# First transform stages of h and K: two matmuls of 64 rows on the two halves of the array's rows, in place of two of 128 rows with zeros

## The chip, the core and the metric

The kernel runs on one core of a Trainium2 chip. The core has TensorE (PE; its weight loads are shown apart as PEld), VectorE (DVE), ScalarE (ACT), GpSimd (POOL) and SyncE (SP), which here only issues DMAs. SBUF is the working memory of 128 partitions, and PSUM, in banks of 128 x 512 f32, takes the results of matmuls. The metric is the device time of one launch in microseconds, lower is better.

## The reference, cut to what matters

One layer with two blocks, on 2048 positions of width D = 640. The change lies in the first block:

```python
h = _layernorm(x) * (1 + ca) + sa
# A block: a long convolution along the positions, for each of the 640 channels
P = exp((A * dt)[:, :, None] * pos)           # 640 x 128 x 2048
K = 2.0 * einsum("dn,dnl->dl", C, P).real     # the filter, 640 x 2048
y = irfft(rfft(h, 2L) * rfft(K, 2L), 2L)[:L]  # + h * D_skip
x = x + ga * y
# B block: x = x + gb * ((silu(h2 @ w1) * (h2 @ w3)) @ w2), h2 a layernorm of x
```

The kernel computes the Fourier transforms as matmuls in stages. The change concerns the first stage of the transform of h and the first stage of that of K.

## The kernel before, in words

Positions are split into 32 outer (t1) and 64 inner (t0) ones. The first stage is a transform over the 32 outer positions, which gives 32 frequencies with a real and an imaginary part, 64 numbers. A tile holds four groups of 32 positions on its 128 partitions (q = 0 to 3). One matmul handles two groups: its 128 output rows are 64 numbers for one group and 64 for the other. The weights for a pair of groups (`pr`, line 268 for h and 574 for K) have 128 rows, and in `shape_tables` only the 64 rows that belong to the pair are filled: rows 0 to 63 for pr = 0, rows 64 to 127 for pr = 1. The others are zeros.

**h.** `h_unit` (lines 248 to 272) does one of eight units: two inner positions j of each group. DVE applies the layernorm to the unit's tile xs (lines 258 and 261, one instruction each for each j), SP loads the unit's weights wa (L254), and then for each pr a tile ho (128 x 2 x 640) is filled: for each j and each half of 320 columns one f32 matmul into a PSUM tile of tag "f" (L268), and an ACT copy from there into ho (L269). Then two DMAs write ho to h1 in DRAM (L272). Buffers: four of xs (XB), two of wa, three of ho (HB), three PSUM tiles of tag "f" (self.fb), which other matmuls share.

**K.** The filter is generated in five pieces of 128 channels (`gen_steps`, `gen_chunk`: POOL and DVE multiply tables, ACT takes sines in lines 489 to 495, PE sums over the 128 states in line 511 into kps, and ACT copies it to ks, L532). `k_steps` (lines 551 to 584) then runs the first transform stage on a piece, in four stages of 16 inner positions: for each pr one f32 matmul of 512 columns (L574), an ACT copy into the tile ko (L576), and after both two DMAs to k1 in DRAM (L581). For the first four pieces each matmul has a PSUM tile "f" of its own. For the last one (`wide`) both write one PSUM tile of two banks (tags "sn" and "cs"), which one ACT instruction copies (L578). ko has two buffers (KB).

`freq_steps` (lines 597 to 630) reads h1 and k1 back (ht and kt, L594) and does the second transform stage (L612 for h, L626 for K), the product on DVE (L628), and the first stage of the inverse (L616). All these have weights of 128 x 128. The second stage of the inverse (L655, and L927 for the first units) uses weights of 128 rows and 64 columns, two matmuls at a time into the two halves of PSUM's partitions (`tile_position`). After this comes the B block (`ffn`), from about 600 us to the end.

**The order of the work** isn't written out by hand. Each step has a priority (`self.at(...)`), and when the program is built a list scheduler with modelled times fixes the order on each engine; on the chip each engine takes its instructions in that order and waits by semaphore. In the h stage the generation of K's first piece runs between the units of h. Some orders are pinned by `self.order`: the h normalisations follow one another on DVE, and the sines on ACT. SP's queue holds the loads of xs, wa and K's parameters and the writes of ho and ko, in one line.

Of the kernel before, what the change touches and what calls it, by code (L numbers as in the profile page):

```python
# [10 lines left out]
F32 = mybir.dt.float32  # L11
F32R = mybir.dt.float32r
I32 = mybir.dt.int32
AF = mybir.ActivationFunctionType
# [4 lines left out]
P = 128  # L19
L = 2048  # L20
D = 640
# [17 lines left out]
HB = int('3')  # L39
# [59 lines left out]
class K:  # L99
# [148 lines left out]
    def h_unit(self, e, ps, u):  # L248
        nc = self.nc
        j0 = u * 2  # L250
        rstd, nm = self.h_rs
        xs = self.xs[u] or self.load_x(e, u, "xs")
        wa = e.tile([P, 2, 2, P], F32, name=f"wa{u}", tag="wa", bufs=2)
        nc.sync.dma_start(wa, self.t_wa[:, j0:j0 + 2])  # L254
        for j in range(2):
            x = xs[:, j, :]
            c = slice(j0 + j, j0 + j + 1)
            i0 = nc.vector.scalar_tensor_tensor(x, x, nm[:, c], self.rA, op0=ALU.add, op1=ALU.mult)  # L258
            if self.hq:
                self.order(i0, self.hq[-1])  # L260
            i0 = nc.vector.scalar_tensor_tensor(x, x, rstd[:, c], self.rB, op0=ALU.mult, op1=ALU.add)
            self.hq.append(i0)
        for pr in range(2):
            ho = e.tile([P, 2, D], F32, name=f"ho{u}{pr}", tag="ho", bufs=HB)
            for j in range(2):
                for o in (0, 320):
                    pt = ps.tile([P, 512], F32, name=f"ph{u}{pr}{j}{o}", tag="f", bufs=self.fb)
                    nc.tensor.matmul(pt[:, :320], wa[:, j, pr, :], xs[:, j, o:o + 320], start=True, stop=True)  # L268
                    nc.scalar.activation(ho[:, j, o:o + 320], pt[:, :320], AF.Copy)  # L269
            for g in range(2):  # L270
                t0 = 16 * (2 * pr + g) + j0
                nc.sync.dma_start(self.h1.rearrange("f r t d -> (f r) t d")[:, t0:t0 + 2, :], ho[g * 64:(g + 1) * 64])  # L272


    def params_begin(self, e):
# [275 lines left out]
    def k_steps(self, pc, st, kop, ps, bufs, wide=None):  # L551

        nc = self.nc
        o0, E, SB = pc * P, E4, 16

        dsk = kop.tile([P, E], F32, name=f"dsk{pc}", tag="dsk", bufs=2)
        nc.gpsimd.memset(dsk, 0.0)
        for q in range(4):
            o = o0 + (2 * (q % 2) + q // 2) * E
            nc.sync.dma_start(dsk[32 * q:32 * q + 1], self.d_skip[o:o + E].rearrange("(o e) -> o e", o=1))  # L560

        def stage(i):
            ks = st["ks"]
            if i == 64 // SB - 1:
                nc.vector.tensor_add(ks[:, 63, :], ks[:, 63, :], dsk)
            ko = (wide if wide and i == 2 else kop).tile([P, SB, 2 * E], F32, name=f"ko{pc}{i}", tag="ko", bufs=1 if wide and i == 2 else bufs)
            kv = ko.rearrange("p s (r e) -> p r s e", r=2)
            if wide:
                pt = ps.tile([P, 2, SB, E], F32, name=f"pk{pc}{i}", tag=("sn", "cs")[i % 2], bufs=1)
            for pr in range(2):  # L570
                if not wide:
                    pt = ps.tile([P, 1, SB, E], F32, name=f"pk{pc}{i}{pr}", tag="f", bufs=self.fb)
                pv = pt[:, pr if wide else 0]
                nc.tensor.matmul(pv, self.wk[:, pr, :], ks[:, i * SB:(i + 1) * SB, :], start=True, stop=True)  # L574
                if not wide:
                    nc.scalar.activation(kv[:, pr], pv, AF.Copy)  # L576
            if wide:
                nc.scalar.activation(kv, pt, AF.Copy)  # L578
            for g in range(2):
                o = o0 + 2 * g * E  # L580
                nc.sync.dma_start(self.k1.rearrange("f r s d -> (f r) s d")[:, i * SB:(i + 1) * SB, o:o + 2 * E],  # L581
                                  ko[g * 64:(g + 1) * 64])

        return [lambda i=i: stage(i) for i in range(64 // SB)]


# [404 lines left out]
```

## Time and profile before

| | us |
|---|---|
| median of 3 runs | 1206.31 (1205.34 to 1208.49) |
| the profiled execution | 1206.96 |
| its span, first to last instruction | 1205.2 |
| PE busy | 1029.8 (85%) |
| DVE busy | 696.6 (58%) |
| ACT busy | 495.2 (41%) |
| POOL busy | 316.6 (26%) |
| L268, matmuls of h, busy in the h stage (83 to 172) | 51.4 |
| L574, matmuls of K, busy | 42.2 |

A busy time is the time in which at least one instruction of the kind ran. "out<-in" names tiles by the program's names: ph and pk are the PSUM tiles of the two first stages, ho and ko the SBUF tiles they are copied to, h and k the DRAM tensors h1 and k1. A number with x counts instructions. "<-" behind an idle time names what ended it. PEclk is the granted clock of TensorE, 1.00 or in tenths of full speed. A line that says "issue" stands for time in which the engine waited for nothing that the profile shows.

### The profile page before, as it was taken

What the parts mean: (1) busy time and instruction counts of PE and PEld (TensorE: products, weight loads), DVE (VectorE), ACT (ScalarE), POOL (GpSimd) and SP (SyncE); (2) the same over time, 40 slices, a digit from 0 to 9 for tenths busy, and PEclk for the clock granted to TensorE, in tenths of its full rate; (3) what the DMA queues carried; (4) which work ended last, traced back from release to release, by engine and by line L of the source; (5) the groups of instructions that cost most, each with busy time, mean ns of one, the idle gap of its engine ahead of it and who ended that gap; (6) DMA issues with size and microseconds to landing.
All of it is one profiled execution on the core that took longest, in us unless ns stands there. A gap on an engine that the chain in (4) does not pass through costs nothing.

```text
span 1205.2 us, 17828 instructions
## 1 busy us (share of the span) xinstructions
PE 1029.8 (85%) x6737; PEld 777.4 (65%) x6737; DVE 696.6 (58%) x1224; ACT 495.2 (41%) x768; POOL 316.6 (26%) x329
## 2 busy tenths in 40 slices
PE   2357673895996989895699999999999999999996
PEld 0134342673775857674376788888888888888885
DVE  7999979746866763143474484544745445354332
ACT  3456566436456573312242243432424333343221
POOL 5677768645757871000000000000000000000000
PEclk9578785797897988998699999999999999999999
DMA  9957648335365454778956333533335332353311
GB/s 265 232 160 222 184 125 220 86 104 116 95 172 112 114 117 122 175 187 218 214 142 155 97 88 88 136 96 86 97 88 133 108 95 74 84 143 98 98 44 44
DMA packets 206525, 157.61 MB, mean 131 GB/s; under 512 B 56680, under 2 KB 188648, under 8 KB 204776
## 3 DMA queue, kind: packets, MB, share of 16 engines
q1 hardware_dynamic: 206440, 156.48, 49.8%
q8 instruction: 53, 0.87, 0.3%
q14 instruction: 32, 0.26, 0.1%
HBM read 119.74 MB, written 36.70 MB: 130 GB/s over the span
## 4 chain that ended last, share of the span: by engine, by line
PE 70%; DVE 14%; DMA 7%; ACT 3%; issue 2%; SPq 2%; POOL 1%; DVEq 0%; ACTq 0%
PE gu L760 11%; PE gu L758 10%; PE gu L759 10%; PE fk L626 6%; PE fa L616 5%; PE acc L793 5%; PE acc L795 5%; PE acc L794 5%; PE fa L612 3%; PE kps L511 3%; PE iy L655 2%; DMA k<-ko 1%; DMA xt<-in_x 1%; DVE xs L258 1%; DVE step L446 1%
## 5 line engine op out<-in xcount | busy, mean ns | idle before, releaser
L758 PE MATMUL gu<-xh,wh 128*128 128x512 f32 x540 | 214.2, 397 | 0.5 <-ACT xh L695 0.5
L760 PE MATMUL gu<-xh,wl 128*128 128x512 f32 x540 | 213.9, 396 | 0.0
L759 PE MATMUL gu<-xl,wh 128*128 128x512 f32 x540 | 213.9, 396 | 0.0
L670 ACT ACTIVATE wh<-wr 128x640 fp32r<-128x640 f32 x108 | 74.2, 732 | 146.7 <-PE gu L759 134.5
L511 PE MATMUL kps<-yy,xx 128*32 128x64 f32 x2560 | 83.5, 247 | 53.3 <-DVE xx L503 28.3
L511 PEld LDWEIGHTS kps<-yy,xx 128*32 128x32 f32 x2560 | 61.6, 123 | 101.4 <-issue 53.9
L727 POOL MEMSET w2l<- 64x640 f32 x4 | 2.5, 626 | 469.0 <-PE acc L794 469.0
L758 PEld LDWEIGHTS gu<-xh,wh 128*128 128x128 f32 x540 | 101.7, 188 | 26.1 <-issue 1.0
L760 PEld LDWEIGHTS gu<-xh,wl 128*128 128x128 f32 x540 | 101.5, 188 | 26.4 <-issue 2.0
L759 PEld LDWEIGHTS gu<-xl,wh 128*128 128x128 f32 x540 | 101.6, 188 | 24.9 <-issue 0.5
L628 DVE TENSOR_TENSOR fp<-fk,hz 128x512 f32<-128x512 f32 x80 | 54.8, 686 | 98.1 <-PE fk L626 97.8
L626 PE MATMUL fk<-kt,wb 128*128 128x128 f32 x640 | 99.8, 305 | 13.1 <-DMA kt<-k 12.3
L626 PEld LDWEIGHTS fk<-kt,wb 128*128 128x128 f32 x640 | 90.6, 212 | 23.8 <-DMA kt<-k 7.6
L793 PE MATMUL acc<-ah,w2h 128*128 128x512 f32 x260 | 104.6, 402 | 0.0
L794 PE MATMUL acc<-ah,w2l 128*128 128x512 f32 x260 | 102.7, 395 | 0.0
L618 ACT ACTIVATE hz<-fa 128x512 f32<-128x512 f32 (+1 forms) x90 | 49.2, 547 | 126.5 <-PE fa L616 105.6
L487 POOL TENSOR_TENSOR yy<-e,e 128x512 f32<-128x512 f32 x80 | 87.0, 1109 | 42.7 <-PE kps L511 42.7
L795 PE MATMUL acc<-al,w2h 128*128 128x512 f32 x260 | 98.1, 395 | 0.0
L671 DVE TENSOR_TENSOR wl<-wr,wh 128x640 fp32r<-128x640 f32 x108 | 84.5, 817 | 16.6 <-ACT wh L670 16.6
L773 DVE SCALAR_TENSOR_TENSOR a<-th,gu 128x512 f32<-128x512 f32 x52 | 35.7, 687 | 100.3 <-ACT th L772 100.2
L774 DVE TENSOR_TENSOR a<-a,gu 128x512 f32<-128x512 f32 x52 | 35.7, 686 | 94.5 <-PE gu L760 94.5
L772 ACT ACTIVATE th<-gu 128x512 f32<-128x512 f32 x52 | 31.1, 598 | 139.5 <-PE gu L760 139.5
(190 smaller groups left out, 1801.2 us busy)
## 6 DMA issues: line engine op xcount, KB each, us to landing
wr<-in_w SPq DMA_DIRECT2D x104, 320.0 KB, 3.9
w2r<-in_w SPq DMA_DIRECT2D x52, 320.0 KB, 3.0
h<-ho SPq DMA_DIRECT2D x32, 320.0 KB, 4.5
k<-ko SPq DMA_DIRECT2D x40, 256.0 KB, 4.3
ht<-h SPq DMA_DIRECT2D x40, 256.0 KB, 2.8
kt<-k SPq DMA_DIRECT2D x40, 256.0 KB, 3.2
zd<-hz SPq DMA_DIRECT2D x80, 128.0 KB, 1.9
wm<-in_w_mod SPq DMA_DIRECT2D x10, 960.0 KB, 8.4
```

What stands on the lines that cost most here:

```text
L487: G.tensor_tensor(out.rearrange("p d (k i) -> p d k i", k=4), bc(t1, 2, 4), bc(t2, 3, 8), op=ALU.mult)
L511: nc.tensor.matmul(kps[q * 32:(q + 1) * 32, e * 64:(e + 1) * 64], xx[:, r, i, :], yy[:, r, i, :, :].rearrange("p a b -> p (a b)"), start=( ...
L616: nc.tensor.matmul(pa[:, 1], self.wz[:, r, :], pp[:, r], start=(r == 0), stop=(r == 1))
L626: nc.tensor.matmul(pk[:, r, g], self.wb[:, 2 * i + g, r, :], kt[:, g0 + g, :], start=True, stop=True)
L670: self.nc.scalar.activation(H, v, AF.Copy)
L671: eng.tensor_tensor(Lo, v, H.bitcast(F32), op=ALU.subtract)
L758: nc.tensor.matmul(pg, wh[:, i, k, :], xh[:, k, :], start=(k == 0), stop=False)
L759: nc.tensor.matmul(pg, wh[:, i, k, :], xl[:, k, :], start=False, stop=False)
L760: nc.tensor.matmul(pg, wl[:, i, k, :], xh[:, k, :], start=False, stop=(k == KT - 1))
L793: nc.tensor.matmul(acc[k], w2h[:, sl], ah, start=(m == 0), stop=False)
L794: nc.tensor.matmul(acc[k], w2l[:, sl], ah, start=False, stop=False)
L795: nc.tensor.matmul(acc[k], w2h[:, sl], al, start=False, stop=(m == 12))
```

## The change

In both places the matmuls take only the 64 rows that are not zeros, weights and data alike: partitions 0 to 63 for pr = 0 and 64 to 127 for pr = 1. The two matmuls of a pair stand next to each other, into two PSUM tiles (in `wide`, two banks of one), and the copies of the pair follow. In `h_unit` the loop over pr becomes the innermost one, so both ho tiles of a unit are taken at its start and filled together, and the four DMAs follow at its end. The tables, the buffers and the priorities stay as they are.

```diff
@@ -260,16 +260,21 @@
                 self.order(i0, self.hq[-1])
             i0 = nc.vector.scalar_tensor_tensor(x, x, rstd[:, c], self.rB, op0=ALU.mult, op1=ALU.add)
             self.hq.append(i0)
+        ho = [e.tile([P, 2, D], F32, name=f"ho{u}{pr}", tag="ho", bufs=HB) for pr in range(2)]
+        for j in range(2):
+            for o in (0, 320):
+                pts = []
+                for pr in range(2):
+
+                    half = slice(64 * pr, 64 * pr + 64)
+                    pts.append(ps.tile([P, 512], F32, name=f"ph{u}{pr}{j}{o}", tag="f", bufs=self.fb))
+                    nc.tensor.matmul(pts[pr][:, :320], wa[half, j, pr, :], xs[half, j, o:o + 320], start=True, stop=True)
+                for pr in range(2):
+                    nc.scalar.activation(ho[pr][:, j, o:o + 320], pts[pr][:, :320], AF.Copy)
         for pr in range(2):
-            ho = e.tile([P, 2, D], F32, name=f"ho{u}{pr}", tag="ho", bufs=HB)
-            for j in range(2):
-                for o in (0, 320):
-                    pt = ps.tile([P, 512], F32, name=f"ph{u}{pr}{j}{o}", tag="f", bufs=self.fb)
-                    nc.tensor.matmul(pt[:, :320], wa[:, j, pr, :], xs[:, j, o:o + 320], start=True, stop=True)
-                    nc.scalar.activation(ho[:, j, o:o + 320], pt[:, :320], AF.Copy)
             for g in range(2):
                 t0 = 16 * (2 * pr + g) + j0
-                nc.sync.dma_start(self.h1.rearrange("f r t d -> (f r) t d")[:, t0:t0 + 2, :], ho[g * 64:(g + 1) * 64])
+                nc.sync.dma_start(self.h1.rearrange("f r t d -> (f r) t d")[:, t0:t0 + 2, :], ho[pr][g * 64:(g + 1) * 64])
 
 
     def params_begin(self, e):
@@ -567,13 +572,18 @@
             kv = ko.rearrange("p s (r e) -> p r s e", r=2)
             if wide:
                 pt = ps.tile([P, 2, SB, E], F32, name=f"pk{pc}{i}", tag=("sn", "cs")[i % 2], bufs=1)
+            pts = []
             for pr in range(2):
                 if not wide:
                     pt = ps.tile([P, 1, SB, E], F32, name=f"pk{pc}{i}{pr}", tag="f", bufs=self.fb)
                 pv = pt[:, pr if wide else 0]
-                nc.tensor.matmul(pv, self.wk[:, pr, :], ks[:, i * SB:(i + 1) * SB, :], start=True, stop=True)
+                pts.append(pv)
+
+                half = slice(64 * pr, 64 * pr + 64)
+                nc.tensor.matmul(pv, self.wk[half, pr, :], ks[half, i * SB:(i + 1) * SB, :], start=True, stop=True)
+            for pr in range(2):
                 if not wide:
-                    nc.scalar.activation(kv[:, pr], pv, AF.Copy)
+                    nc.scalar.activation(kv[:, pr], pts[pr], AF.Copy)
             if wide:
                 nc.scalar.activation(kv, pt, AF.Copy)
             for g in range(2):
```

## The prediction

> **What bounds the kernel now.** I read the busy shares in 40 slices first, then the busy time by stretch, then the groups by line, the chain of work that ended last, and single stretches of the timeline. Durations come from the profiled execution: 1206.96 us, of which the span is 1205.2, so 1.8 us lie around it. The median of the timed runs is 1206.31, 0.65 less; the sum is made against 1206.96.
>
> ```profile
> PE   2357673895996989895699999999999999999996
> DVE  7999979746866763143474484544745445354332
> PEclk9578785797897988998699999999999999999999
> ```
>
> One slice is 30 us. From slice 20 on, PE is full; the change doesn't touch that half. The matmuls of h (L268) lie in slices 2 to 5, those of K (L574) between 172 and 498 us.
>
> ```profile
> core 0: us, PE busy (x) PEld busy (x) DVE busy (x) ACT busy (x) POOL busy (x), PEclk, DMA share, GB/s
> 83.00:172.00 89.00, 62.18 (x567) 38.05 (x569) 87.44 (x121) 56.30 (x109) 61.53 (x52) 0.81 0.57 161
> 172.00:221.00 49.00, 23.56 (x343) 15.28 (x335) 40.59 (x72) 27.57 (x45) 40.95 (x46) 0.67 0.67 186
> 460.00:510.00 50.00, 45.81 (x344) 35.15 (x342) 12.70 (x20) 14.44 (x22) 1.02 (x2) 1.00 0.59 143
> ```
>
> In the h stage (83 to 172 us) DVE is busy 87.4 of 89 us and PE 62: DVE is the bound. From 460 to 510 PE is (45.8 of 50); there lie the K matmuls of the last piece of D.
>
> ```profile
> L268 PE MATMUL ph<-xs,wa 128*128 128x320 f32 x128 | 51.4, 543 | 16.8 <-DVE e L448 4.4 <-issue 3.1 <-DMA h<-ho 2.5
> L269 ACT ACTIVATE ho<-ph 128x320 f32<-128x320 f32 x64 | 26.5, 435 | 19.1 <-PE ph L268 16.8 <-DMA h<-ho 0.6 <-PE kps L511 0.6
> L574 PE MATMUL pk<-ks,wk 128*128 128x512 f32 x80 | 42.2, 641 | 4.0 <-DVE ks L565 3.7 <-ACT ko L576 0.3
> L576 ACT ACTIVATE ko<-pk 128x512 f32<-128x512 f32 x32 | 18.3, 596 | 16.4 <-DMA k<-ko 8.2 <-PE pk L574 8.1
> ```
>
> 128 records for 64 matmuls, 80 for 40: each f32 matmul makes two passes. The mean is latency, not pace. Pace: 12 passes of L268 at 140.05 took 3.47 us, so (3.47 - 0.43)/11 = 0.28 us each; at the half clock (16 passes in 7.52 us at 128.48) about 0.5. A pass of L574 goes at 3.44/8 = 0.43 us, by the chain below.
>
> ```profile
> 271.03 1.07 PE pk L574 x2
> 272.12 0.61 ACT ko L576
> 273.39 4.32 DMA k<-ko
> ...
> 487.77 3.44 PE pk L574 x8
> 494.26 1.72 PE pk L574 x4
> 496.41 1.72 PE pk L574 x4
> ```
>
> Columns: start, length in us. These are K's matmuls on the chain: their eviction and write in the second piece, and PE itself in the last.
>
> **Do two halves really run together?** No 64-row matmul is in this trace. The nearest row is the inverse transform, whose two matmuls use 64 columns each, on two halves of the columns:
>
> ```profile
> 604.85 1.84 PE L655 MATMUL iy<-iz,wd 128*64 128x320 f32 x12
> ```
>
> Twelve passes one after another would need 12 x 0.27 = 3.2 us; they took 1.84, which is six steps of 0.27 and a tail. So I take a pair of halves at the time of one matmul. The bounds are that and no overlap at all (third rival).
>
> **The change, part by part.** The number of passes, evictions and DMAs stays. What changes: two passes share one step; both matmuls of a pair come before both evictions; and in h both tiles of a unit fill together, with the four writes after all eight evictions instead of two after four.
>
> K, piece by piece of D, on the chain:
> - First piece (168 to 184 us, DVE busy 6.1 of 16): six passes are on the chain, 172.55 for 2.77. A pair and one half of the next pair take four steps: 2 x 0.43 = **-0.9**. Ends 0 and -1.3 (full halving).
> - Second piece: the evictions start at 270.18 and 272.12, the second 1.07 us idle for its matmul. Paired, it follows the first by the 0.48 at which such evictions run back to back, or the 0.60 of one: 272.12 - 270.78 = 1.3 earlier, less 0.2 for the start of the pair: **-1.1**. Next late are the write (4.3 us) and ACT's table work, which move along.
> - Third piece: the evictions are at 353.69 and 356.34, with other ACT work between. Ends 0 and -2.0 (353.69 + 0.60 against 356.34, less 0.2 and some); nearest to ACT being busy (13.4 of 20 us), so **-0.5**.
> - Fourth piece (430 to 453): ACT is busy 19.7 of 23 us, and the chain goes through ACT and two k writes. The four first evictions spread over 432.10 to 437.35; unspread, they would end 2.7 earlier. Ends 0 and -2.7, I take **-1.0**.
> - Last piece: 3.44 + 1.72 + 1.72 = 6.88 on the chain, halved: -3.44. Against it stand changes of shape. In this trace, going from a 128-column matmul to a 64-column one left 0.10 us after the last pass plus 0.05 for weights no longer loaded ahead (518.46 to 518.55), and coming back 0.10 plus 0.10; with 128 columns to load it is 0.2 each way. Three groups cost 3 x 0.4 = 1.2: **-2.2**, ends 0 and -3.4.
>
> Sum for K: -0.9 - 1.1 - 0.5 - 1.0 - 2.2 = **-5.7 us**.
>
> The Trainium skill (TensorEngine Tiling (Array Packing), Key Properties) says that a change of tiling mode drains the engine. For column halves the gaps just named agree; whether row halves count as a mode, no run here shows. By that rule the last piece is -2.2, without it -3.4.
>
> h: 64 matmuls lose half of 128 x 0.27 = 34 us of PE streaming, but DVE's 87.4 of 89 us covers it. Only one stretch of the chain there is PE (128.48, 6.46 us, 12 passes at the half clock); halved it gives 3.2 at most, and DVE has its own queue at that time, busy to 137. Against it stands the buffer of ho. There are three. Tile 2 of a unit needs the place of tile 1 of the unit before. Its writes used to be issued half a unit ahead of that unit's end; now they come behind its last eviction.
>
> ```profile
> DMA to landing us min/median/max: 4.2/4.5/5.5
> ```
>
> The place is free 0.6 (second issue, L272) + 4.5 = 5.1 us after the unit's end. The next unit's second eviction now stands some 1.5 us behind it (units one and two: 98.2 and 99.38). So ACT can stall up to 3.6 us at seven changes of unit, 25 us in all, against 89 - 56.3 = 32.7 us that it has idle here. Behind the eviction in ACT's queue stand the sines (L489, L495), and DVE waits for those. Before, 3.1 us of waits for these writes (0.6 on ACT, 2.5 on PE) went with 1.6 us of DVE idle. Ends -3.2 and +12.6 (half the stall reaches DVE); I take **+1.5**, as if that idle doubled.
>
> The Trainium skill (same page, PSUM Bottleneck) says that tiling speeds TensorE but not the emptying of PSUM. Here a pair of h would take 0.54 us on PE, and its two evictions run 0.32 apart when back to back, 0.64 in all. By that rule h gains a little less on PE; as DVE bounds the stage, the sum is the same but for the half clock.
>
> Sum: 1206.96 - 5.7 + 1.5 = **1202.8 us**.
>
> **Rivals.**
> - *The ho buffers decide (slower).* Place: ACT's queue between units of h. If half of the 25 us gets through to DVE: -5.7 + 12.6 = +6.9, 1213.9. It decides once more than 9.3 us (5.7 + 3.6) of the stall, or 37%, passes through. For it: DVE has no slack. Against: the order of ACT's queue is planned with the wait known, so sines can go first.
> - *The K gain is swallowed.* In pieces two to four other engines (ACT, the writes) end as late as before: -0.9 - 2.2 + 1.5 = -1.6, 1205.4. For it: ACT's 19.7 of 23 us.
> - *The halves don't run together:* no gain, the changes of shape and the buffers remain: +1.2 + 1.5, 1209.7. Against: the column halves.
> - *All of it shows:* K at its far ends (-1.3 - 1.3 - 2.0 - 2.7 - 3.4 = -10.7), and h at -3.2: 1193.1.
>
> **How the numbers follow.** About 0.3% (3.6 us) is what a measurement of this kernel tells from no change. Forecast (1199 to 1203.3) 0.36; all of it 0.10; swallowed 0.17; no overlap 0.05; buffers 0.32. Faster 0.36 + 0.10 = 0.46, same 0.22, slower 0.32. The forecast's own range is 1199 to 1203.3. The whole range, 1195 to 1213, leaves out the far end of the first case (0.05) and the upper half of the last (0.15).
>
> **What would show it.** Right: twelve or more passes of L268's successor at a step of 0.27 per pair; pk groups of the last piece at half of 6.88 us; the second eviction of a stage right behind the first. The buffers: idle time of ACT's ho eviction released by "DMA h<-ho" of 10 us and more, and DVE busy well under 87 in a longer h stage. Wrong: pairs that start 0.43 apart, or an order of DVE's work so changed that its stretches between 172 and 221 us grow or shrink by more than K's terms; that I can't work out from this trace.

## The result and the profile after

The changed kernel takes 1241.36 us (median; 1240.14 to 1242.94) beside 1207.05 (1205.34 to 1208.49) for the kernel before on the same chip: a ratio of **1.0286**, 95% interval [1.0266, 1.0305]. It is slower by 34 us, outside the predicted range of 1195 to 1213. The profiled execution took 1240.14 us, its span is 1238.3.

The busy shares in 40 slices, now of 31 us each:

```profile
PE   2356787579499797979389999999999999999996
DVE  7999842953873866324355466454745435354442
PEclk9975555589789798989689999999999999999998
```

Slices 3 to 7, the h stage, stand at a granted clock of 0.5 or a little over, where before had 8, 7, 8, 5 and 7 tenths. From slice 21 on TensorE is full in both. The busy time by stretch (columns: stretch, its length, then busy us with the number of instructions on PE, PEld, DVE, ACT and POOL, the granted clock, DMA share, GB/s):

```profile
83.00:172.00 89.00, 61.67 (x421) 31.27 (x422) 74.27 (x112) 43.05 (x82) 55.38 (x48) 0.51 0.38 111
172.00:221.00 49.00, 41.20 (x275) 19.58 (x273) 18.61 (x37) 27.09 (x51) 21.74 (x26) 0.53 0.40 118
```

The first stretch was bound by DVE before: 87.44 busy. Now DVE is busy 74.27 of 89, and every engine got through fewer instructions (ACT 82 instead of 109, PE 421 instead of 567). The second stretch is new ground: PE is busy 41 of 49 us where it had 23.56, with work of h that before had finished. The last write of h is issued at 213.1 us; before, it was at 172.8. K's first-stage matmuls start at 206.0 us (before 172.5) and their last eviction starts at 531.4 (before 498.2), both some 33 us late, so the 34 us are lost ahead of them.

The chain of waits from the end of the first stretch on, start and length in us:

```profile
163.55 1.43 PE ph L271 x2
164.98 0.58 PE kps L516 x8
165.56 1.36 PE ph L271 x2
```

TensorE itself is on the chain: one matmul of h (two passes of 64 rows, at the half clock), a group of kps, one matmul of h, and so on up to 206 us, broken by one wait of ACT for a write of h (184.6 to 188.7). The two halves of a pair, which were to run side by side, stand apart with kps between them. In the trace of before kps also stands between single matmuls in places (111.9 to 116.5 us), but elsewhere it holds runs of 4 to 18 passes of ph.

The waits that grew, from the groups by line of the window 83 to 221 us (busy us, mean ns, then idle us before the instruction and what ended it):

```profile
L271 PE MATMUL ph<-xs,wa 64*128 64x320 f32 x128 | 71.1, 797 | 28.6 <-ACT ho L273 23.3 <-DVE e L453 4.8 <-DVE xs L261 0.5
L273 ACT ACTIVATE ho<-ph 128x320 f32<-128x320 f32 x64 | 25.2, 431 | 33.3 <-PE ph L271 20.7 <-DMA h<-ho 12.6
L373 ACT ACTIVATE pp_at<-pp_k 128x128 f32<-128x128 f32 x1 | 0.3, 309 | 10.2 <-DVE pp_k L372 10.2
```

DVE bounded the first stretch before, so its waits are where to look for the loss. Its longest waits between 83 and 221 us, first before, then after (us in total, times, longest):

```profile
DVE e L448 <- ACT E L341: 7.8, 1, 7.8
```

```profile
DVE e L453 <- ACT E L346: 21.8, 1, 21.8
DVE yy L504 <- POOL yy L492: 16.1, 3, 5.9
DVE xs L258 <- DMA xs<-in_x: 4.8, 2, 2.8
```

The lower two don't occur before. The three add up to 42.7 us, 34.9 more than the 7.8 of before: the size of the loss. The longest is for E, the exponentials of K's next piece; ACT computes them from a transpose (ptp) that TensorE does at 204.4 us, at the end of the row of ph and kps above (before: at 179.0). The loads of xs that DVE waits for stand in SP's queue behind writes of h; the last is issued at 156.7 us, before at 123.7.

So the suspects are the ho buffers of the prediction (12.6 us), an arctan that waits 10.2 us in ACT's queue, GpSimd's yy, which waits for kps, and the late E. The mean of a pass of ph rose from 543 to 797 ns.

### The profile page after: what moved, and what is told of

Read it like the earlier page. It is cut to its first block, busy times and chain, and to the rows that moved or that the text cites. A ratio compares the mean times of both kernels' runs of the same rounds, so it can differ in the third digit from the quotient of the medians.

```text
span 1238.3 us, 17833 instructions
## 1 busy us (share of the span) xinstructions
PE 1053.5 (85%) x6737; PEld 775.1 (63%) x6737; DVE 688.0 (56%) x1224; ACT 495.8 (40%) x768; POOL 315.8 (26%) x329
## 4 chain that ended last, share of the span: by engine, by line
PE 71%; DVE 10%; DMA 10%; SPq 3%; ACT 3%; issue 2%; POOL 1%; DVEq 0%; ACTq 0%
PE gu L768 10%; PE gu L770 10%; PE gu L769 10%; PE fk L636 7%; PE fa L626 5%; PE acc L803 5%; PE acc L805 5%; PE acc L804 5%; PE kps L516 3%; PE fa L622 3%; DMA xt<-in_x 2%; PE ph L271 2%; DMA k<-ko 2%; PE iy L665 2%; DVE xs L258 1%
## 5 line engine op out<-in xcount | busy, mean ns | idle before, releaser
L516 PEld LDWEIGHTS kps<-yy,xx 128*32 128x32 f32 x2560 | 68.4, 132 | 111.0 <-issue 70.3
L516 PE MATMUL kps<-yy,xx 128*32 128x64 f32 x2560 | 95.7, 263 | 39.3 <-DVE xx L508 12.2
L636 PE MATMUL fk<-kt,wb 128*128 128x128 f32 x640 | 96.6, 298 | 18.4 <-DMA kt<-k 11.1
L636 PEld LDWEIGHTS fk<-kt,wb 128*128 128x128 f32 x640 | 87.4, 206 | 28.7 <-issue 9.1
L271 PE MATMUL ph<-xs,wa 64*128 64x320 f32 x128 | 71.1, 797 | 28.6 <-ACT ho L273 23.3
```

Source lines behind the costliest of these rows:

```text
L271: nc.tensor.matmul(pts[pr][:, :320], wa[half, j, pr, :], xs[half, j, o:o + 320], start=True, stop=True)
L516: nc.tensor.matmul(kps[q * 32:(q + 1) * 32, e * 64:(e + 1) * 64], xx[:, r, i, :], yy[:, r, i, :, :].rearrange("p a b -> p (a b)"), start=( ...
L636: nc.tensor.matmul(pk[:, r, g], self.wb[:, 2 * i + g, r, :], kt[:, g0 + g, :], start=True, stop=True)
```

## Experiments: what was told apart

Theories after the result. **Order:** the kernel is emitted with a planner that sets the order on every engine (the kernel builds its TileContext with schedule_with_timeline_sim); with 64 rows in h it set another order, and that order is the loss. **Buffers:** the loops are the loss, through the ho writes (the prediction's rival). **Clock:** passes of 64 rows hold the clock at half, and that is the loss.

To tell them apart, a kernel can be held to the order of another one. A short function behind emit takes, for each engine, the list of instruction names in the order of that other build, and ties each to the one ahead of it by a dependence without a semaphore, so that nothing is added that runs:

```
+    dep = mybir.DependencyInfo(mybir.DependencyClass.NoSync, mybir.DependencyReason.DATA)
+    for names in json.loads(zlib.decompress(base64.b85decode(ORDERS))):
...
+        for a, b in zip(names, names[1:]):
+            tc.add_manual_dep(have[b], a, dep, reason="order")
```

### Rows and order, each alone

The label full_after_plan is the changed loops with 128 rows in the planner's own order for them; full_after_plan_pinned is the same held to the order of the changed kernel. The edit of both:

```
-  nc.tensor.matmul(pts[pr][:, :320], wa[half, j, pr, :], xs[half, j, o:o + 320], start=True, stop=True)
+  nc.tensor.matmul(pts[pr][:, :320], wa[:, j, pr, :], xs[:, j, o:o + 320], start=True, stop=True)
```

and the same for pk. rows_before_plan is the reverse: the loops of before with 64 rows for h and K, held to the order of before (the line of h; K's is cut in the same way):

```
-  nc.tensor.matmul(pt[:, :320], wa[:, j, pr, :], xs[:, j, o:o + 320], start=True, stop=True)
+  nc.tensor.matmul(pt[:, :320], wa[64 * pr:64 * pr + 64, j, pr, :], xs[64 * pr:64 * pr + 64, j, o:o + 320], start=True, stop=True)
```

rows_in_full_plan is the changed kernel, unedited, held to the order that the planner gave to its 128-row version (full_after_plan).

> The loops of the kernel before, with its order on every engine pinned instruction by instruction, but each first-stage matmul of h and K takes 64 rows. Clock theory (64-row passes do not lift TensorE's granted clock as 128-row passes do): the h stage runs at 0.5 to 0.6 in place of 0.81, and the kernel is 10 to 25 us slower than before. Order theory (the loss comes from the order of the planner, which sets kps groups between the halves): within 4 us of before, 1203 to 1211. Buffer theory (the ho tiles): also within 4 us, since ho is used as before.

> The loops of the changed kernel with matmuls of 128 rows, as before, and the order left to the planner. Clock theory: the clock stays near 0.8 in the h stage, 1205 to 1215. Buffer theory: both ho tiles of a unit still fill together, so most of the 34 us remain, 1230 to 1241. Order theory: depends on where the planner puts kps; with halves of 128 rows it should leave the ph groups together, 1205 to 1215.

> Matmuls of 128 rows in exactly the order that the changed kernel has on every engine. Clock theory: 128-row passes lift the clock even with kps between them, so well under 1241: 1210 to 1225. Order theory and buffer theory: both causes are kept, so 1235 to 1245.

> The changed kernel's own loops and 64-row matmuls, but pinned to the order that the planner chose for the same loops with 128 rows (1.003 of before), where ph stands in groups of 5 to 13. Plan theory: 1200 to 1215. If it is the 64-row shape on the chip that costs (clock, changes of shape): 1225 or more.

Measured, as ratios to the kernel before on the same chip:

| loops, order held to | 128 rows | 64 rows |
|---|---|---|
| loops and order of before | 1 (the kernel before) | 1.0051 [1.0031, 1.0071] |
| changed loops, planner's order for 128 rows | 1.0031 [1.0008, 1.0053] | 1.0026 [1.0008, 1.0043] |
| changed loops, order of the changed kernel | 1.0239 [1.0206, 1.0273] | 1.0286 [1.0266, 1.0305] |

Down a column, the bad order (that of the changed kernel) costs 2.1% with 128 rows and 2.6% with 64 over the good one (the planner's for 128 rows); across a line, the 64 rows cost nothing or half a per cent. The planner's order with 128 rows costs 0.3% although both ho tiles of a unit fill together there too, which speaks against the buffers. The run of 64 rows in the order of before falls between its ranges: the clock in its h stage is 0.54, as the clock theory has it, but the time is 6 us longer, under the 10 to 25 of that theory and over the 4 of the others. The 128-row kernel in the bad order shows the waits of the changed one. Two of its waits between 83 and 172 us (us in total, times, longest):

```profile
PE ph L271 <- ACT ho L273: 28.2, 14, 9.2
ACT pp_at L373 <- DVE pp_k L372: 10.1, 1, 10.1
```

And the changed kernel in the good order has the stretch back (columns as above):

```profile
83.00:172.00 89.00, 72.33 (x580) 40.28 (x580) 87.30 (x121) 53.81 (x105) 63.91 (x54) 0.56 0.50 153
```

DVE 87.30 beside before's 87.44, 580 passes beside 567; but a granted clock of 0.56 beside 0.81. So the clock falls with 64 rows in the good order as well, and there the time doesn't follow, since DVE bounds the stage. The order theory holds for the loss of more than 2%; the clock theory holds at most for the half per cent between 1.0239 and 1.0286, and between 1 and 1.0051.

DVE's three waits follow the order as well. In the 128-row kernel in the bad order they are 18.1, 14.0 and 4.4 us, 28.7 more than before, and the 2.39% by which it is slower are 28.8 us; in the changed kernel in the good order only the wait for E is there, with 10.3 us. TensorE's row of ph, on the other hand, is 19.9% of the chain between 83 and 221 us in the changed kernel and 3.9% with 128 rows in the same order, with nearly the same loss: in the bad order DVE is kept waiting whether TensorE is on the chain or not.

### h alone, K alone

k_own_plan and h_own_plan have one hunk of the diff each, in the planner's own order. rows_own_plan has the loops of before with 64 rows in both, in the planner's own order. k_rows_before_plan has 64 rows in K alone, in the loops and the order of before; in the last piece K's two matmuls of a pair stand next to each other there already, in the pieces before mostly not:

```
-  nc.tensor.matmul(pv, self.wk[:, pr, :], ks[:, i * SB:(i + 1) * SB, :], start=True, stop=True)
+  nc.tensor.matmul(pv, self.wk[64 * pr:64 * pr + 64, pr, :], ks[64 * pr:64 * pr + 64, i * SB:(i + 1) * SB, :], start=True, stop=True)
```

> Only K's part of the change, loops and rows, the order left to the planner; h as before. My sum gave K -5.7 us. If the gain of the pairs in K is taken back by the loads that follow (as in the run with before's order, 1.000 of before): 1203 to 1209. If the planner also breaks the pairs of K or shifts the pieces: 1210 to 1225. A version worth keeping would be below 1202.

> Only h's part of the change, the order left to the planner; K as before. If the loss comes from the h stage alone: 1235 to 1245, as the whole change. If K's part holds some of it: 1215 to 1230.

> The loops of the kernel before with 64-row matmuls, the order left to the planner; against the run with the order of before pinned (1.005 of before) only the plan differs. Plan theory (the 64-row shape makes the planner set kps groups between single ph matmuls, and that order costs some 30 us): 1230 to 1245. Loop theory (that order hurts only together with the two ho tiles filled at once): 1208 to 1218.

> Only K's first stage with 64 rows, in exactly the order of before on every engine. My sum gave K -5.7 us. In this order most K matmuls stand alone between kps groups, so only neighbouring halves can overlap: in the last piece all, elsewhere few. Overlap theory: the last piece -2 to -3 us, in all 1201 to 1204 against 1206. Clock theory: a rise of the clock is put off by a window of 3.4 us at some of the five pieces, 0 to +4.

Measured: K's part alone 1.0011 [0.9993, 1.0028], h's part alone 1.0295 [1.0266, 1.0324]. The loss is all in h. Rows without the change of loops: 1.0182 [1.0148, 1.0215] where the planner was free, 1.0051 in the order of before. So the shape of the matmul alone, with nothing moved in the source, made the planner choose an order that costs over a per cent (one of its four runs, at 1220.55 us, lies 10 us under the others); and the changed loops with 128 rows got one that costs 0.3%. Why the planner chooses so was not looked into.

K in the order of before: 0.9998 [0.9983, 1.0014], so the 2 to 5 us that the overlap was expected to bring in all don't show. The chain of its profile in the last piece, to be read beside the three pk rows of before (3.44, 1.72 and 1.72 us):

```profile
486.17 1.92 PE pk L574 x8
488.09 0.63 PE fa L612 x2
...
491.33 1.06 PE pk L574 x4
492.39 0.63 PE fa L616 x2
493.02 1.06 PE pk L574 x4
494.08 1.09 PE fk L626 x8
...
499.30 0.50 SPq L581
499.85 0.67 SPq L581
500.61 1.43 SPq L621
502.13 1.26 SPq L594
...
503.49 0.51 SPq L621
...
504.61 4.61 DMA kt<-k
509.36 2.04 PE fk L626 x8
```

The same places before:

```profile
491.21 0.43 PE fa L612 x2
...
495.98 0.43 PE fa L616 x2
...
498.13 0.89 PE fk L626 x8
...
505.93 0.46 SPq L621
...
507.00 4.23 DMA kt<-k
511.36 2.05 PE fk L626 x8
```

1.92 + 1.06 + 1.06 = 4.04 where before had 6.88: the halves run together. But the group behind each of the three takes 0.20 us longer (0.63 for 0.43, twice, and 1.09 for 0.89), so of 2.84 us some 2.2 are saved on TensorE. And what ends the piece is the load of kt, behind five DMA issues in SP's queue (SPq, 499.30 to 504.00, 4.4 us of them on the chain, beside 0.46 before). From the first pk to the fk that needs kt it takes 509.36 - 486.17 = 23.19 us, before 511.36 - 487.77 = 23.59. Of the 2.2 us, 0.4 are left. In k_own_plan, too, the way from the first pk to that fk is 23.24 us (487.60 to 510.84); there the chain goes through the write of k and then the load of kt.

### The buffers of ho

after_plan_four_ho is the changed kernel, held to its own order, with four buffers of ho:

```
-HB = int('3')
+HB = int('4')
```

> The changed kernel in its own order on every engine, pinned, with four ho buffers in place of three. Buffer theory (inside this order ACT stands at ho evictions until the writes of ho have landed, 12.6 us shown, and PE and DVE behind it): 1215 to 1228. If the order loses its time elsewhere (the arctan of the parameters, which waits 10 us for DVE; changes between ph and kps): 1233 to 1241.

Measured: 1.0283 [1.0259, 1.0307]. In the window 83 to 221 us the evictions' line is

```profile
L273 ACT ACTIVATE ho<-ph 128x320 f32<-128x320 f32 x64 | 25.0, 430 | 23.1 <-PE ph L271 23.1
```

The 12.6 us of waits for the writes of h are gone, and the time is what it was; that of DVE for E is 21.9 us beside 21.8. The buffers theory falls. The sign that the prediction had named for it (10 us and more of waits for "DMA h<-ho", with DVE well under 87) was there all the same: what DVE waits for was late anyway.

### Which place of the order

Two runs hold the changed kernel to the good order (that of full_after_plan) on some engines only, and leave the rest to the planner: on TensorE alone, or on VectorE, ACT, GpSimd and SyncE.

> The changed kernel with PE's order alone pinned to that of the good order (that of the same loops with 128 rows, in which the changed kernel ran at 1.003 of before); the other engines are planned anew around it. If kps groups between the halves of ph on PE are what costs: 1205 to 1218. If it is the order on ACT and DVE (an arctan that holds ACT for 10 us): 1225 to 1241.

> The reverse: ACT, DVE, POOL and SP pinned to the good order, PE left to the planner, which again sets kps groups between ph matmuls. If the interleaving on PE is what costs: 1225 to 1241. If the other engines' order does: 1205 to 1218.

Measured: 1.0197 [1.0166, 1.0227] and 1.0155 [1.0129, 1.0182], against 1.0026 with all of them. Neither is enough. On the engines left free the planner set a new order, which is neither the good nor the bad one, so these two runs don't divide the loss between the engines. The first lies in the range named for the order on ACT and DVE, the second between its two ranges.

Two runs take the changed kernel's own order and move only five instructions on ACT: the arctan with the two behind it, and the two abs, stand behind the next evictions of ho; in the second with four ho buffers as well:

```
 order of ACT, changed kernel:  ... pp_at pp_s pp_m  ho ho ...    abs abs  ho ho ho ...
 order of ACT, moved:           ... ho ho  pp_at pp_s pp_m ...    ho ho ho  abs abs ...
```

> The changed kernel in its own order on every engine, but on ACT each arctan and the two instructions behind it (L373, L379, L380) stand behind the two following evictions of ho, and each two abs (L365, L366) behind the three following ones. Theory 1, ACT's in-order queue: in the changed kernel ACT waits 10.19 us for pp_k at an arctan with evictions of ho behind it, and TensorE has 23.3 us of waits for ACT's ho; if that is where the order loses, this run is 4 to 10 us under the changed kernel, a ratio of 1.020 to 1.026 against the kernel before. Theory 2, the loss is spread over the places of kps between the passes of ph and over DVE's order: within 3 us of the changed kernel, a ratio of 1.026 to 1.031.

> The same order as the run beside it, with four buffers of ho instead of three. Theory 1: with ACT's queue free, the next wait of the evictions is the one for the write of h (12.6 us in 3 waits in the changed kernel), and this run is another 3 to 8 us under the run beside it. Theory 2: within 2 us of the run beside it, as four buffers alone gave 1.0283 beside 1.0286.

Measured: 1.0295 [1.0259, 1.0332] and 1.0276 [1.0238, 1.0314]. Nothing is won: theory 2 holds for the first, and the second lies 2.2 us under it, within the noise. The wait only changes its name. Of ACT's waits between 83 and 172 us in the first of the two:

```profile
ACT sn L494 <- DVE xx L506: 13.4, 5, 4.3
ACT ho L273 <- DMA h<-ho: 8.9, 2, 5.7
ACT pp_at L373 <- DVE pp_k L372: 5.2, 1, 5.2
```

The last two runs change only TensorE's order, in its place of ph: the second matmul of a pair moves up behind the first (pairs), or all four matmuls of one j stand together (fours):

```
 order of PE, changed kernel:  ph(lo) kps.. ph(hi) kps.. ph(lo) kps.. ph(hi) kps..
 pairs:                        ph(lo) ph(hi) kps.. kps.. ph(lo) ph(hi) kps.. kps..
 fours:                        ph(lo) ph(hi) ph(lo) ph(hi) kps.. kps.. kps.. kps..
```

> The changed kernel in its own order on every engine, but on TensorE the second matmul of each pair of ph stands right behind the first, ahead of the groups of kps that the order had put between them. Theory 1, the halves that kps separates don't run together: with the pairs together TensorE's part of the stage falls by about half of the 64-row passes that stood alone, some 30 of 64 matmuls at half of 2 x 0.8 us, and this run is 5 to 20 us under the changed kernel, a ratio of 1.012 to 1.025. Theory 2, what costs is that kps comes late for GpSimd and VectorE, whoever stands ahead of it: within 4 us of the changed kernel, a ratio of 1.025 to 1.032.

> As the run beside it, with the four matmuls of ph of one j together, as few groups of kps between them as in the kernel before. Theory 1: at most 3 us under the run beside it, since the halves run together in both. Theory 2: kps still later, so the same or up to 6 us over the changed kernel.

Measured: 1.0248 [1.0223, 1.0273] and 1.0255 [1.0232, 1.0278]. The lines of ph of the first, of the page, and a stretch of its timeline on PE (start, length, instruction, idle before):

```profile
L271 PE MATMUL ph<-xs,wa 64*128 64x320 f32 x128 | 57.4, 757 | 37.8 <-ACT ho L273 32.4
```

```profile
166.11 2.15 PE L271 MATMUL ph<-xs,wa 64*128 64x320 f32 x4
168.19 1.07 PE L516 MATMUL kps<-yy,xx 128*32 128x64 f32 x26
169.20 1.44 PE L271 MATMUL ph<-xs,wa 64*128 64x320 f32 x4
```

Where the halves run side by side, a pair now takes 1.44 us where one of them took 1.43. But only about a dozen of the 32 pairs do: between the halves of many others TensorE waits for an eviction of ACT, or the second starts late (the 2.15 us above). ph's busy time fell by 13.7 us, from 71.1 to 57.4. The time fell by 0.4% (4 to 5 us of 34; the two intervals overlap a little), and DVE's wait for E with it, from 21.8 to 16.4 us: 9.1 us of the 13.7 came back as waits for ACT's evictions (23.3 before the move, 32.4 after). The run lies just where the two expectations meet, and so confirms neither in full: bringing those pairs together regains some 0.4%, and the rest of the loss stays. What all pairs side by side would bring in this order was not measured.

### Does a pass of 64 rows lift the clock?

clock_blocks, of which there is one execution, is the kernel before with six blocks of TensorE work behind its end, each behind 13 us of idle TensorE: 24 f32 matmuls (48 passes) of 320 columns with 128 rows; with 128 rows and weights half of them zeros, as in h before; with 64 rows alone (partitions 0 to 63); with pairs of 64 rows on both halves (96 passes); with 64 columns; with pairs of 64 columns (96). The core of the edit:

```
+  kinds = (("full", [(A, R, A)]), ("zeros", [(A, self.wk[:, 0, :], A)]), ("half", [(U, R, A)]),
+           ("pair", [(U, R, A), (L_, R, A)]), ("col", [(A, R, U)]), ("colpair", [(A, R, U), (A, R, L_)]))
...
+  nc.tensor.matmul(pg[cols, :320], w[rows, cols], t[rows, :320], start=True, stop=True, **kw)
```

> The kernel before, and behind its end six blocks of matmuls of 320 columns on data, each after some 11 us of idle PE: 24 of 128 rows; 24 of 128 rows with half of the weights zeros; 24 of 64 rows on one half; 24 pairs on both halves of the rows; 24 on one half of the columns; 24 pairs on both halves of the columns. The blocks add work whose output is not used. Clock theory: the first two reach full clock after 4 to 8 us (passes go from 0.53 to 0.27 us), the block of 64 rows alone stays at 0.53 for its whole length (25 us), and the pairs, if both halves run together, rise again. Other theories: all blocks rise alike.

The four blocks with all columns in the timeline, and their granted clocks by stretch in the same sequence (stretch, length, PE busy with the number of passes, granted clock, DMA):

```profile
1210.17 14.81 PE L833 MATMUL bfull<-bt,x 128*128 128x320 f32 x48 [13.77 <-ACT bt L826]
1238.32 16.09 PE L833 MATMUL bzeros<-bt,wk 128*128 128x320 f32 x48 [13.34 <-ACT bt L826]
1267.75 25.96 PE L833 MATMUL bhalf<-bt,x 64*128 64x320 f32 x48 [13.34 <-ACT bt L826]
1307.05 16.81 PE L833 MATMUL bpair<-bt,x 64*128 64x320 f32 x96 [13.34 <-ACT bt L826]
```

```profile
1210.17:1224.98 14.81, 14.81 (x48) 0.89 0.00 1
1238.32:1254.41 16.09, 16.09 (x48) 0.82 0.00 0
1267.75:1293.71 25.96, 25.96 (x48) 0.50 0.00 0
1307.05:1323.86 16.81, 16.81 (x96) 0.84 0.00 1
```

64 rows alone stay at half the clock for all 26 us and take 25.96/48 = 0.54 us a pass. Every other block starts at the half clock and is lifted within it, after 3.3 us (128 rows) to 6.0 us (64 columns, 0.81 over the block; their pairs have 0.87). Pairs do 96 passes in 16.81 us, within 5% of the 48 passes with zeros. So halves of the rows overlap in full, and the clock rises for them in this block, where they stand side by side; a half by itself runs at half speed. In the h stage (83 to 172 us) pairs together brought the clock only from 0.51 to 0.53, and fours to 0.55.

The Trainium skill (TensorE: Matmul & The Clock Gate, Part 1) states that the clock rises after a busy window of about 3.4 us. The full block agrees (lifted after 3.3 us); the block of 64 rows doesn't: 26 us of unbroken passes were not enough.

## Why the prediction was wrong, point by point

- **What bounds the stage** was right: DVE, 87.4 of 89 us. As long as the order keeps DVE fed, little that TensorE does there shows: 580 passes at a clock of 0.56 gave 1.0026.
- **The failed step is the pricing of h at the order of before.** "I take +1.5, as if that idle doubled" moved seven changes of unit in a queue that was otherwise taken as it stood. The kernel's order isn't written in its source around the change: a planner sets it for every engine, and a matmul with 64 rows makes it set another. That cost is 1.0286 against 1.0026 with the good order, 2.6%, some 31 us; h alone measured 1.0295, some 35 us where the prediction had +1.5. The prediction named "an order of DVE's work so changed" in its last paragraph as what would make it wrong, for the stretches between 172 and 221 us, gave it no price and no chance, and so had a range without it. What the runs showed in place of the +1.5: not a stall at the changes of unit, but DVE, which bounds the stage, waiting 34.9 us more for E, yy and xs. A bound was to be had from two rows of the trace of before, at the end of its h stage, where a single matmul of ph (at the half clock) and a group of kps stand one behind the other:

```profile
170.38 1.44 PE L268 MATMUL ph<-xs,wa 128*128 128x320 f32 x2
171.74 0.80 PE L511 MATMUL kps<-yy,xx 128*32 128x64 f32 x28
```

  From the one start to the next it is 1.36, and with kps (up to pk at 172.48) 2.1 us. If all 64 matmuls of h went so, they would take 64 x 2.1 = 134 us and end at 217 instead of 172, +45 us. That is a bound and not what happened: in the changed kernel 27 of the 64 were left at 163 us, 17 of them alone between groups of kps (1.36 + 0.58 each), and the 128-row kernel lost nearly as much in that order.
- **The ho buffers** were weighed as the rival that ends slower, at 1213.9. The sign came (12.6 us of waits, DVE at 74.27), the cause didn't: four buffers remove the wait and leave 1.0283, and the same loops with 128 rows in the planner's order cost 0.3%.
- **Pairs run together** was right where they are adjacent: 4.04 for 6.88 us in K's last piece, and 16.81 us for 96 passes in the block. The prediction's -2.2 for TensorE in that piece was right in both its parts: halving gives -3.44, and the three changes of shape cost 0.60 in the groups of pk and 0.60 in the groups behind them, the 1.2 that it had. The drain that the Trainium skill states for a change of tiling mode (TensorEngine Tiling (Array Packing), Key Properties) agrees with those 0.2 us each way; that it is a drain no run tells from another cost of the change. In h they were not adjacent, which the prediction had not asked: its source puts them side by side, TensorE's queue doesn't.
- **K's sum of -5.7** failed: 0.9998 [0.9983, 1.0014] in the order of before excludes a gain of more than 2 us, and 1.0011 [0.9993, 1.0028] with K's changed loops one of more than 1. In the last piece the sum took TensorE's saving for the whole, with nothing late behind it: the DMAs of k, and in the order of before SP's queue, take back all but 0.4 us. In the second piece the second eviction was to follow right behind the first; in k_own_plan the two start at 267.30 and 269.43, no closer than before (270.18 and 272.12), since there, too, the pair's matmuls start apart (266.14 and 268.27). The rival "The K gain is swallowed" is what K did, and more so, since it had kept the first and the last piece. How the other pieces divide was not measured by itself.
- **The clock** entered only as durations. That a lone half doesn't lift it was not foreseen. It is worth at most about half a per cent here (1.0239 to 1.0286, and 1 to 1.0051), and nothing in the good order (1.0031 and 1.0026), where DVE hides it.

What stays open: which place of the order holds the 2.6%. With TensorE alone, or the others alone, in the good order a part comes back (1.0197, 1.0155); the pairs that could be brought together are some 0.4% of it; ACT's arctan and the ho buffers show none. DVE's waits for E, yy and xs account for the loss: in the six runs that hold the whole or nearly the whole of the bad order their growth between 83 and 225 us and the loss agree within 3.1 us. But that is an account and not an experiment: no run moved the transpose for E, kps ahead of GpSimd, or SP's loads of xs by themselves. Open is also why the planner decides as it does.

None of these kernels is faster than the kernel before; the nearest are K alone (0.9998 and 1.0011) and the changed kernel in the good order (1.0026).

## What to carry to other kernels

Where a planner orders the queues, a change of an instruction's shape is a change of the order of everything around it: give "the order comes out otherwise" a price and a chance of its own, by asking how long the stage is if the engines run their parts one after another. When such a change disappoints, hold the new kernel to the old order and the old one to the new before looking at any single wait: here the two most visible waits (12.6 us for the ho buffers, 10.2 us for the arctan) could be taken away or halved without moving the time, since they were waits of ACT; the waits of DVE, the engine that bounds the stage, are the ones that added up to the loss. And halving the time of an engine that doesn't bound the stage wins nothing, even where the mechanism works as meant.

## What the hardware showed that was not expected

- Passes of 64 rows alone never lifted the granted clock: 0.50 over 25.96 us, beside 0.82 to 0.89 for 128 rows, with zeros or without, 0.84 for pairs of halves, and 0.81 for 64 columns with all rows (one execution).
- Two halves of the rows, f32, cost as much as one full matmul: 16.81 us for 96 passes beside 14.81 to 16.09 for 48.
- The stretch of h kept a clock of 0.51 in the changed kernel and 0.56 in the good order, with TensorE busy 72.33 of 89 us; 128 rows in the bad order, busy 56.40, had 0.70. Being busy isn't what decided; how many rows were at work went with it.
- Going from 128 rows to pairs of 64 and back cost 0.2 us each way in K's last piece (0.60 in three groups of pk, 0.60 in the groups behind them).
